# Two more theta tiles on split operands, under a new written-out order, in an attention and mixing kernel

## The chip, the cores and the metric

The kernel runs on one core of a Trainium2 chip. The metric is the device time of one execution in microseconds. Five engines work side by side, each through its own list of instructions in a fixed order: TensorE (PE, with its weight loads shown as PEld), VectorE (DVE), ScalarE (ACT), GpSimd (POOL), and SyncE (SP), which here only issues DMAs. An instruction starts when the one before it on its engine has left and the semaphores that it waits for have come.

## The reference

The first half is an attention over a sliding window and over block sums; the second half mixes its result along the sequence and along the channels. With 4 batches, 8 heads, 768 positions and 64 values per head, `x` is 768 x 512 per batch:

```python
    k_sum = k.reshape(B, H, nb, block, D).max(axis=3)      # block = 32
    v_sum = v.reshape(B, H, nb, block, D).mean(axis=3)
    scores_l = scale * np.matmul(q, k.transpose(0, 1, 3, 2))  # kept where |s - t| < 16
    scores_s = scale * np.einsum('bhsd,bhnd->bhsn', q, k_sum) + np.log(block)
    ...                                       # softmax over both, times v and v_sum
    theta = x @ w_theta
    zr, zi = x * np.cos(theta), x * np.sin(theta)
    y = np.einsum('ts,bsd->btd', w_tok_r, zr) + np.einsum('ts,bsd->btd', w_tok_i, zi)
    u = x + y
    return u + np.maximum(u @ w_ch, 0.0)
```

Everything is float32 in the result. The weights arrive as float64 and are made into float32 on the chip.

## The kernel before, in words

**Tiles.** Each batch has six tiles of 128 positions, so there are 24 tiles, numbered 0 to 23; batch 0 has tiles 0 to 5. For each tile the kernel does in turn: scores on PE (L538), mask, scale and row minimum on DVE (L574, eight pairs of instructions), exponentials on ACT (L578, eight), transposes of the result on PE (L587), their copies to SBUF on ACT or DVE (L593), the product with the values on PE (L561), and its normalisation (L602 to L611), which gives `xn`, the tile of `x`. Then `x` is turned: for the first six tiles by PE transposes (L638), later through DRAM. Then comes theta (L672 or L677), its reduction to one turn and cosine and sine (L688 to L701), and the product with `x` (L707), called `zu`.

**Two ways to multiply.** A float32 product of full precision is done raw (L672), with float32 operands, in which each matmul shows as two records in the trace; or on split operands (L677): each operand is cast to a rounded part (the high part, L311 or L313) and the rest is kept as a second part (the low part, a subtraction, L320), and three matmuls high x high, high x low, low x high take the place of the raw one. In the table `TUNE`, `RT` is the number of the first tile whose theta is done on split operands: 6 before. From that tile on, `x` of the tile is split into `xh` and `xl`. The split weights of theta, tiles `wth`, are made from the float32 weights, which lie until then in the same four buffers of the tags `xh` and `xl`.

**Mixing.** Each batch is mixed over the sequence in six steps for each half of the channels: raw for the first four steps of batch 0 (L735 with the operand `zu`), on split operands (L735 with `hl`) until batch 1 is done, and for batches 2 and 3 by a scheme with seven products in the place of eight (L851). The channel product of all batches ends the program (L956), with its sums on DVE (L963) and the final relu and sum (L975), each of which is stored.

**Order.** Nothing is scheduled on the chip or by the compiler. The kernel records some 2330 operations, and `ORDER`, a written-out list of their numbers, gives the one order in which all of them are issued; the letter behind a number (p, a, d, g) chooses PE, ACT, DVE or POOL where an operation can run on more than one, and without a letter the cheapest by the kernel's own costs is taken. Each engine runs its instructions in that order. All DMAs go through the one queue of SP, also in that order, and one that waits for a buffer holds up all behind it. An instruction of POOL that the kernel marks with `port` also waits for the last marked instruction of DVE, if that was issued just before it among the marked ones.

Of the kernel before, what the change touches and what calls it, by code (L numbers as in the profile page):

```python
# [54 lines left out]
27 23 25 15 31 39 17 24 29 99 44 28 33 0g 1g 2 35 78 3 45 4 186 40 85 26 193 43 8g 5 6g 9 30 10 11g 18 19 7g 194 20 21 22 32  # L55
12 48g 47 14 46 49 50 13 190g 237g 100 101g 34 239 59 63 235 51 60 52 64 61 65 238g 192 36 92 54 58 56 53 79 55 102 62 187 57
103 37 38g 104 105d 66 691d 67 80 81 82 42g 188g 83 191 68 195 41 291g 69d 70 196 189g 240g 84 71 86 87g 293 199 106 107 198
197 204 206 294g 207 200 203 205 685g 241 72 75d 289 73 210 76 208 74d 202 77d 88 93 223 236 201 211 209 347g 242 245 249 94
224 243 244 345g 247 89 212 213 215 214 246 225 248 216 117 95 220 90 96 91d 97 346g 250 397 348g 98 226 217d 251 252 108 253
218 221 254 227 256 219d 118g 292g 222d 122 119 228 123 255 258 257 124 229 230 689g 120 259 260 295 261 296 269 121 262 419g  # L60
125 231 109 298 270 263d 232 302 126 233 398 266 343 264 271 304 405 272 687g 273 274 290 399 128 692g 307 267 281 265d 311
268d 275 297 306 110 282 305 299 421g 301 309 276 349 285g 300 303 310 406 308 129g 350 352 234g 353 312 130 277 354 131 313
283 323 315 400 111 416 314 133 316 351 358 409 324 325 420 418 284 360 287g 278 317 362 134g 355 135 356 364 132 326 136 327
357 359 363 137 328 279g 344 401 288g 280 361 365 329 320d 403 422 318 321 319d 322d 410 431 366 367 138 686g 434 438 330 433
335 368d 337 331 417 377 688g 402 432 601g 369 332 404 378d 370 116 139g 338 476 690g 423 426 430 477 371d 374d 424 372 437
375 379 425 429 373d 376d 380 140 411 381 334 407 141 428 142 286g 113 16 427 439 436 435 527 440 441 442 478 602 382 172
333g 412 443 383 479 482 408 528 447d 444d 487 445 489 336 143 491 389 144g 448 112 384 173g 446 449d 488 524 486 490 153 413
494 493 145 414 174 146 492 114 391 450 473 483 480 484 481 485 415g 529 147 495 525 115 148 390 175 385 526 392 149g 386 154
475 127 451d 530 474 150 496 155 497 151 498 452 176 453 454 455 152 156 158 387 157 456 499 177 727 533 457 500 532 388g
503d 572 501 504 159g 178 538 458 459 502d 464 460g 506 466 540 505d 165 467 507 539 508 693 509 537 531 535 510 536 543 534  # L70
160 541 542 545 694 544 697 511 695 728 166g 167 179 462 512 161 546 547 168 573 162 169 696 463g 465 163 180 698 549 513 170
548d 164 514 515 699 181 171 550 182 516 518 608 522 554 183 523 700g 393 519 520 184 729 521 574 551 517g 575 561 341g 607
582 584 394g 576 461g 559 731 588 701 555 702 185 585 730 637 571 580 560 733 562 557 719 552 553 577 558g 732 579 581 703
1238 563 583 556 768 578 713g 734 569 565 771 589 586 342 609 339g 340g 769 590 587 720 567 591 592 704 564 638g 735 593 603
468g 736 1239 770 594 595 618 705 706 621 610 611 615 470 620 772 598 1240 613 617 612 1241 625 599 721 722 469g 773 723 395g
396 774 596 622 597d 600 604 800 624 605 639 606 641 642 619 647 640 645 775g 776 616 614 626 623 627 643 714 650 724 725
471g 679g 629d 568 644g 824g 628 651 630 566 802 803 707 472 631 632 825 708 634d 801 660 826 661 827 828g 829g 739 652 655
804 805 726 662 777 649 635 737g 710 666 709 646 656 653 681 654 680 682 658 778 779 780 830d 633 648 683 684 832 636d 781
715 947 716 711g 659 570 664 831 657 668 665 977 806 663 834g 667 807 669 835 833 670 836g 740 981 671d 672 673d 738 980 717
837g 838 712 808 839 978 741 979 782 783 844 749 809 948 718 750 982 676 840 842 745 944 945d 785 752 784 674 677 756 753  # L80
841g 743 1028g 742 675d 678 810 811 812 744 748 746 983g 984g 788 751 843 790 813 755 791 1242 845 747 1001 814 754 757 758
760 815 1002 796 759d 786d 949 846 761 765 789 787 1003 958 959 963 854g 961 965 950 855g 762d 962 763 792 985 1005 816 951
856g 1004 794 798 766 1029 986 987 988 952 820 954 953 1243 989 990 797 817g 847g 848 818d 849g 1006 819 764d 955 960 991 767
992 946 850d 793 1007d 957 821 822 1087 823 997 1058 964 998 999 1008 1009 1000 956 966 967 969 852 1023 1030 1061 1059 968
1060 970 994 851 864g 865g 853 857 858 1062 1021 1025 993 995 859 860g 866 867 1010 1039 1022 1031 861g 799 795 1034 1011 971
1063 862 1042 1024 1038 1032 1036 1033 1137 974 1043 972 1035 1041 973d 868 869g 975 976d 1214 870g 1045 1040 1012 1037 1026
1046 1047 1064g 1065g 863 1044 1048 1050d 1027 1013 1049 1014 1088 1051 1215 871 1015 1089 1218 1091 1216 996g 874g 875 1066
1016 1052d 1086 1217 1017g 1093 873 1097 1099 1055d 1053 1056 1019g 1020g 1100 872 876g 1103 1067 1068 1069 1095 1219 1070
1092 1220g 1018 1101 1090 1094 1080 1081 1098 1054d 1136 1096 1078 1079 1102 877g 1246 1057d 1287 1104 1105 1106 1107 1250
1138 1082 1083 1290 1288 1071 1072d 1108 878 1109 1247 1289 1221g 1166g 1222 1073 1074 1110d 1113 1114 1076d 1223 1147 1224  # L90
1225 1291 1292 1151 1075g 1226 1251 1111 879g 1252 1139 1084 1142 1141 1112 1085 1077 1148 1248 1293d 1294g 1227 1140 1115
1317 1253 1120 1143 1118 1116 1179 1130 1144 1119 1249 880 1150 1146 1258 1149 1121 1128 1167g 1145 1154 1295 1296 1254 1255
# [83 lines left out]
class Program:  # L176
# [5 lines left out]
    WINDOW, WARM, COOL = 3.41, 0.88, 0.45  # L182
# [971 lines left out]
```

## Time and profile before

| what | value |
|---|---|
| median of 3 runs | 426.37 us |
| the 3 runs | 426.08, 426.37, 429.6 us |
| the profiled execution | 425.32 us |
| its span, first to last instruction | 423.6 us |
| PE busy | 413.3 us, 98% of the span |
| PE weight loads busy | 343.9 us, 81% |
| DVE busy | 356.3 us, 84% |
| ACT busy | 298.1 us, 70% |
| POOL busy | 207.4 us, 49% |
| DMA moved | 100.07 MB |
| granted TensorE clock | 1.000 |

A busy share is a mean over the whole span, and stages differ: a matmul's end is modelled and lies after the start of the next, so that PE reads as busy wherever matmuls follow each other without a pause.

### The profile page before, as it was taken

To read this page: it belongs to the slowest core of one execution; us is meant where nothing else is said; L and a number is where in the kernel's file an instruction comes from. 1 tells how busy PE (TensorE), PEld (TensorE's weight loads), DVE (VectorE), ACT (ScalarE), POOL (GpSimd) and SP (SyncE) were. 2 spreads that over 40 slices of the span, in tenths; PEclk is the share of its full clock that TensorE was granted. 3 is DMA by queue.
4 is the path that set the end of the run, shared out by engine and by line. 5 is a ranking of instruction groups with operands and counts; after the bars stand their busy time and mean duration, and the time that the engine had idled before them with its cause. 6 is when DMAs were issued, how large, how long until landed. Compare 5 with 4: busy or idle time off the path is not lost.

```text
span 423.6 us, 10058 instructions
## 1 busy us (share of the span) xinstructions
PE 413.3 (98%) x3626; PEld 343.9 (81%) x3626; DVE 356.3 (84%) x963; ACT 298.1 (70%) x609; POOL 207.4 (49%) x211
## 2 busy tenths in 40 slices
PE   8789999999999999999999999999999999999996
PEld 3356666578888888888888899898889999999996
DVE  3799999998797896787778787776887899999996
ACT  2899999997588886878779976685564547465230
POOL 3435562329833545875755876835515411133241
PEclk9999999999999999999999999999999999999999
DMA  8999799567869799777896998998788599111355
GB/s 294 351 351 319 256 384 285 157 212 193 273 181 245 177 261 277 223 241 230 227 271 166 310 248 244 303 267 249 182 242 336 192 349 305 50 39 45 124 209 183
DMA packets 95234, 100.07 MB, mean 236 GB/s; under 512 B 41936, under 2 KB 80848, under 8 KB 95184
## 3 DMA queue, kind: packets, MB, share of 16 engines
q1 hardware_dynamic: 95184, 99.43, 76.0%
q8 instruction: 28, 0.46, 0.4%
q14 instruction: 22, 0.18, 0.1%
HBM read 75.82 MB, written 23.59 MB: 235 GB/s over the span
## 4 chain that ended last, share of the span: by engine, by line
PE 88%; DVE 7%; ACT 2%; issue 1%; DMA 1%; DVEq 0%; SPq 0%; ACTq 0%
PE m L735 23%; PE m L851 20%; PE t L677 11%; PE c L956 6%; PE pa L561 6%; PE m L956 5%; PE s L538 5%; PE t L672 4%; PE pa L587 3%; PE t L381 2%; PE t L956 1%; DMA v<-vg 1%; DVE e L574 1%; DVE x L975 1%; DVE f L763 1%
## 5 line engine op out<-in xcount | busy, mean ns | idle before, releaser
L851 PE MATMUL m<-wt,hl 128*128 128x384 f32 x504 | 93.0, 339 | 0.3
L851 PEld LDWEIGHTS m<-wt,hl 128*128 128x128 f32 x504 | 87.2, 188 | 3.5 <-issue 0.5
L735 PE MATMUL m<-wt,hl 128*128 128x512 f32 x480 | 89.4, 340 | 0.0
L735 PEld LDWEIGHTS m<-wt,hl 128*128 128x128 f32 x480 | 74.2, 188 | 11.6 <-issue 0.3
L578 ACT ACTIVATE e<-e,st 128x118 f32<-128x118 f32 x192 | 64.4, 389 | 10.6 <-DVE st L574 7.3
L574 DVE CUSTOM_DVE_ANT_0 e<-s,cs 128x118 f32<-128x118 f32 x192 | 45.6, 271 | 7.1 <-PE pa L561 4.5
L320 POOL TENSOR_TENSOR hl<-zu,hl 128x512 fp32r<-128x512 f32 x24 | 33.1, 1386 | 27.8 <-ACT hl L311 8.5
L677 PE MATMUL t<-wth,xh 128*128 128x512 f32 x144 | 45.8, 399 | 0.0
L707 POOL TENSOR_TENSOR zu<-xn,zu 128x512 f32<-128x512 f32 x24 | 32.9, 1381 | 21.2 <-DVE wt L414 10.0
L311 ACT CAST hl<-zu 128x512 fp32r<-128x512 f32 x43 | 26.1, 619 | 16.4 <-PE m L851 9.9
L561 PEld LDWEIGHTS pa<-v,e 118*64 118x64 f32 x768 | 24.6, 137 | 9.7 <-issue 3.4
L320 DVE TENSOR_TENSOR hl<-zu,hl 128x512 fp32r<-128x512 f32 x38 | 28.3, 751 | 3.0 <-ACT hl L311 2.9
L561 PE MATMUL pa<-v,e 118*64 118x65 f32 x768 | 28.0, 224 | 2.7 <-ACT xh L1031 1.0
L677 PEld LDWEIGHTS t<-wth,xh 128*128 128x128 f32 x144 | 25.2, 188 | 4.5
L677 PE MATMUL t<-wth,xl 128*128 128x512 f32 x72 | 28.4, 394 | 0.0
L763 POOL TENSOR_TENSOR zu<-zu 128x512 f32<-128x512 f32 x14 | 18.8, 1357 | 16.2 <-DVE hl L320 10.9
L763 POOL TENSOR_TENSOR f<-f 128x192 f32<-128x192 f32 x26 | 17.4, 670 | 18.2 <-DVE f L763 11.2
L538 PE MATMUL s<-k 64*64 64x118 f32 x768 | 25.7, 266 | 0.6 <-PE pa L561 0.6
L593 ACT COPY e<-pa 118x512 f32<-118x512 f32 x30 | 16.7, 584 | 13.4 <-PE pa L587 13.4
L578 ACT ACT_TABLE_LOAD x18 | 23.1, 1283 | 2.7 <-DVE st L574 2.5
L700 ACT ACT_TABLE_LOAD x19 | 24.4, 1283 | 0.3
L593 DVE COPY e<-pa 118x512 f32<-118x512 f32 x18 | 12.2, 688 | 14.5 <-PE pa L587 8.4
(181 smaller groups left out, 891.0 us busy)
## 6 DMA issues: line engine op xcount, KB each, us to landing
wt<-s_scratch SPq DMA_DIRECT2D x48, 384.0 KB, 5.1
k<-qg SPq DMA_DIRECT2D x18, 632.0 KB, 5.7
v<-vg SPq DMA_DIRECT2D x24, 390.0 KB, 5.5
s_scratch<-f SPq DMA_DIRECT2D x24, 384.0 KB, 3.5
wt<-wtr SPq DMA_DIRECT2D x6, 768.0 KB, 10.5
wt<-wti SPq DMA_DIRECT2D x6, 768.0 KB, 11.7
f<-kT SPq DMA_DIRECT2D x12, 384.0 KB, 3.6
f<-vT SPq DMA_DIRECT2D x12, 384.0 KB, 4.8
```

Of the source, the lines that this page charges most:

```text
L320: lambda e: V[e].tensor_tensor(dst(), src(), hi().bitcast(F32), op=ALU.subtract), reads, writes, due, port=BOTH)
L538: mm(0.79 * len(pairs) / NP, [lambda p=p, g=g, h=h: nc.tensor.matmul(sc[h].get()[ROW[g], p], q()[ROW[h], p, ROW[g]], keys_of()[ROW[h], :, ...
L561: mm(2 * 0.433 + scores[0] + (0.2 if scores[0] else 0.0), [lambda n=n, g=g, a=a: nc.tensor.matmul(xa[a].get()[ROW[g], n], turned[g].get()[ ...
L574: op({"DVE": 0.205}, lambda eng, n=n: nc.vector.tensor_tensor_reduce(e()[:, n], sc[n % 2].get()[:, 2 * a + n // 2], mask(m), -SCALE, 3.0e3 ...
L578: op({"ACT": 0.288}, lambda eng, n=n: nc.scalar.activation(e()[:, n], e()[:, n], AF.Exp, bias=st.get()[:, n:n + 1], scale=-1.0), [(st, n)] ...
L593: lambda e, t=t, g=g: (nc.scalar.copy if e == "ACT" else nc.vector.tensor_copy)(t.get()[:NK], tp[g].get()[:NK].rearrange("k n q -> k (n q) ...
L677: calls = [lambda t=t, xx=xx, k=k, c=c: nc.tensor.matmul(th.get(), xx.get()[:, c], w_th[c].get()[:, k], start=(c == 0 and t == 0), stop=(c ...
L707: op({"DVE": c_dve(DM, "two"), "POOL": c_pool(DM)}, lambda e, z=z, hc=hc: V[e].tensor_tensor(z(), xn[b, i].get().rearrange("p h d -> p (h ...
L735: nc.tensor.matmul(acc[th](), zz, w[:, TT[th]], start=(s == 0 and r == 0 and t == 0 and (th == 0 or c == 0)), stop=(s == NT - 1 and r == 1 ...
L763: lambda e: V[e].tensor_tensor(dst(), x(), y(), op=ALU.add if sign > 0 else ALU.subtract), reads, writes, due, port=BOTH)
L851: calls = [lambda ref=ref, tt=tt, z=z, s=s, j=j, t=t, x=x, k=k, bank=bank, first=first: nc.tensor.matmul(bank[j].get()[:, :HT], z.get()[:, ...
L956: calls = [lambda k=k, t=t, x=x, y=y: nc.tensor.matmul(to.get(), weights[n][x][0]()[:, k, j * P:(j + 1) * P], operands[n].get()[:, y, k], ...
```

## The change

`RT` goes from 6 to 4: theta of tiles 4 and 5 (the fifth and sixth of batch 0) is done on split operands, as that of all later tiles already was. Each of the two loses four raw matmuls (eight records) and gets twelve on split operands, one cast and one subtraction. All of `ORDER` is written anew (two of its lines are shown), with four more numbers, 2336 in place of 2332; nothing else in the file differs. A few operations change their engine with it: of the 48 multiplications of L707, 24 stood on DVE and 24 on POOL, and 30 and 18 stand there now; ACT gets 36 table loads in place of 38. The number of DMAs, 317, is the same.

```diff
 ORDER = """
-27 23 25 15 31 39 17 24 29 99 44 28 33 0g 1g 2 35 78 3 45 4 186 40 85 26 193 43 8g 5 6g 9 30 10 11g 18 19 7g 194 20 21 22 32
...
+27 17 31 23 25 14 0 29 1g 8 9 10 2 3 15 16 4 5 13 39 44 33 18 19 20 21 48 35 78 186 45g 40 85 99 24 26 43 28 11g 30 46g 194g
...
 TUNE = dict(R_W2=0.0, PS_T=1, XHB=2, FB=3, FC=2, R_M=49.3, R_C=20049.4,
             R_W=72.0, R_PRE=-11.25, R_KV=14.48, R_SM=-38.05, R_AV=27.7, R_TH=-7.23, R_Z=16.22, R_Z2=-31.01, R_X=0.0, XT=1, XNB=3, A0=3,
-            A1=13, T1=10, PREP=5, VSPE=1, VB=2, KB=2, STR=2, WARM=5, SP0=1, FUSE=99, RELOAD=2, RT=6, RM=4, XA=6, XB=2, ZU=5, HL=4, EB=3, TAU_A=8.2, TAU_M=4,
+            A1=13, T1=10, PREP=5, VSPE=1, VB=2, KB=2, STR=2, WARM=5, SP0=1, FUSE=99, RELOAD=2, RT=4, RM=4, XA=6, XB=2, ZU=5, HL=4, EB=3, TAU_A=8.2, TAU_M=4,
```

The first place is the head of SP's queue, the loads with which the program begins (`kT` and `qg` hold keys and queries, `vn` the values for the block sums, `wth` the raw weights of theta, `vg` the values). Before:

```order
L305 DMA zu<-kT 128x798 x3
L305 DMA x<-vn 128x2x512
L305 DMA k<-qg 128x512
L305 DMA zu<-kT 128x798
L305 DMA wth_91<-wth 128x1024
L305 DMA x<-vn 128x2x512 x2
L305 DMA wth_103<-wth 128x1024
```

Now:

```order
L305 DMA zu<-kT 128x798
L305 DMA x<-vn 128x2x512
L305 DMA zu<-kT 128x798 x3
L305 DMA k<-qg 128x512
L305 DMA x<-vn 128x2x512 x2
L305 DMA wth_123<-wth 128x1024
```

The last of the four key loads moved up from sixth to fifth place, and the second and third load of `vn` stand ahead of the first weights.

The second place is the head of ACT's list. Before:

```order
L506 ACT_TABLE_LOAD
L506 COPY k<-zu 128x47x2x2 x3
L519 COPY k<-ks 128x12x2x2 x2
L506 COPY k<-zu 128x47x2x2 x2
L519 COPY k<-ks 128x12x2x2 x2
L403 ACTIVATE xl<-wth_91 128x512
L506 COPY k<-zu 128x47x2x2
L578 ACTIVATE e<-e,st 128x118 x3
```

Now:

```order
L374 ACT_TABLE_LOAD
L374 ACTIVATE loaded<-beps 128x1
L506 COPY k<-zu 128x47x2x2 x2
L519 COPY k<-ks 128x12x2x2 x2
L506 COPY k<-zu 128x47x2x2 x3
L578 ACTIVATE e<-e,st 128x118 x6
```

The first table load now belongs to an operation that needs no DMA, and the first conversion of weights (L403) moved behind the first exponentials. On PE, which has no rows here, the scores of tile 1 moved ahead of the transposes of tile 0 (they stood behind them), and the product with the values of tile 0, the turning of its `x` and the transposes of tile 1 now follow each other, with the scores of tile 2 behind them (these stood ahead of the turning).

The third place is PE at theta of tile 4. Before, behind the transposes of tile 6 (the last row of which stands first):

```order
L587 MATMUL pa_1025<-cs,e 118x64
L672 MATMUL t<-xh,x 128x512
L672 MATMUL t<-xl,x 128x512
L672 MATMUL t<-xh,x 128x512
L672 MATMUL t<-xl,x 128x512
L561 MATMUL pa_1087<-v,e 64x65 x8
```

Now, behind the scores of tile 7:

```order
L538 MATMUL s_1059<-k 64x118
L677 MATMUL t<-wth_417,xh 128x512 x2
L677 MATMUL t<-wth_417,xl 128x512
L677 MATMUL t<-wth_465,xh 128x512 x2
L677 MATMUL t<-wth_465,xl 128x512
L677 MATMUL t<-wth_700,xh 128x512 x2
L677 MATMUL t<-wth_700,xl 128x512
L677 MATMUL t<-wth_498,xh 128x512 x2
L677 MATMUL t<-wth_498,xl 128x512
L735 MATMUL m_629<-wt,zu 128x512
```

Four raw matmuls became twelve on split operands; theta of tile 5 is changed in the same way.

## Rows read from the trace of the kernel before

**Rows 1.** Page, busy time of each engine, its share and its instructions.

```profile
PE 413.3 (98%) x3626; PEld 343.9 (81%) x3626; DVE 356.3 (84%) x963; ACT 298.1 (70%) x609; POOL 207.4 (49%) x211
```

**Rows 2.** Windows: length, then busy time of PE, PEld, DVE, ACT, POOL, clock, DMA.

```profile
0.00:30.00 30.00, 24.50 (x225) 11.78 (x226) 20.60 (x85) 19.74 (x53) 12.28 (x37) 1.00 0.96 328
30.00:90.00 60.00, 59.46 (x604) 35.72 (x604) 58.31 (x169) 58.73 (x117) 28.20 (x28) 1.00 0.82 275
90.00:120.00 30.00, 30.00 (x303) 25.08 (x300) 25.75 (x70) 21.25 (x53) 21.38 (x18) 1.00 0.84 238
120.00:355.00 235.00, 234.36 (x2131) 206.84 (x2130) 187.56 (x541) 170.11 (x343) 124.36 (x116) 1.00 0.84 248
355.00:424.00 69.00, 65.01 (x374) 64.53 (x373) 64.05 (x103) 28.26 (x48) 21.20 (x12) 1.00 0.35 122
```

**Rows 3.** Chain that ended last: start, length in us, what; theta tiles on PE.

```profile
72.93 3.65 PE t L672 x8
...
145.15 2.79 PE t L677 x12
...
168.97 3.00 PE t L677 x12
```

**Rows 4.** Waits of PE over the span: total us, times, longest.

```profile
PE t L381 <- DVE zu L379: 1.6, 1, 1.6
PE pa L561 <- ACT xh L1031: 1.0, 1, 1.0
PE pa L561 <- DVE e L593: 0.9, 2, 0.5
PE pa L587 <- ACT vs L475: 0.8, 1, 0.8
PE pa L561 <- issue: 0.6, 1, 0.6
PE s L538 <- PE pa L561: 0.6, 1, 0.6
PE pa L452 <- DMA x<-vn: 0.4, 1, 0.4
PE t L672 <- ACT x L311: 0.4, 1, 0.4
```

**Rows 5.** Timeline of PE in the head: start, length, instruction, [idle before].

```profile
12.41 3.61 PE L452 MATMUL pa<-x,vt 128*24 128x512 f32 x8 [0.44 <-DMA x<-vn]
16.80 0.68 PE L587 MATMUL pa<-cs,e 64*118 64x64 f32 x16 [0.77 <-ACT vs L475]
17.40 1.08 PE L538 MATMUL s<-k 64*64 64x118 f32 x32
19.45 1.24 PE L561 MATMUL pa<-v,e 118*64 118x65 f32 x32 [0.97 <-ACT xh L1031]
21.24 1.48 PE L538 MATMUL s<-k 64*64 64x118 f32 x32 [0.55 <-PE pa L561]
```

**Rows 6.** Timeline of ACT in the head.

```profile
6.18 1.28 ACT L506 ACT_TABLE_LOAD   x1 [6.18 <-DMA zu<-kT]
...
17.71 0.57 ACT L593 COPY e<-pa 118x512 f32<-118x512 f32 x1
```

**Rows 7.** Groups by line and shape: busy us, mean ns | idle before, releaser.

```profile
L707 DVE TENSOR_TENSOR zu<-xn,zu 128x512 f32<-128x512 f32 x24 | 19.4, 817 | 3.6 <-ACT zu L701 3.5
L611 DVE TENSOR_TENSOR xn<-pa,st 128x256 f32<-128x256 f32 x35 | 13.8, 415 | 1.9 <-POOL zu L707 1.6
L604 DVE RECIPROCAL st<-st 128x4 f32<-128x4 f32 x48 | 7.6, 170 | 0.4
L320 POOL TENSOR_TENSOR xl<-x,xh 128x512 fp32r<-128x512 f32 x8 | 10.6, 1321 | 11.4 <-DVE f L414 4.8 <-DVE st L574 2.1 <-DVE f L763 1.8
L707 POOL TENSOR_TENSOR zu<-xn,zu 128x512 f32<-128x512 f32 x24 | 32.9, 1381 | 21.2 <-DVE wt L414 10.0 <-ACT zu L701 4.9 <-DVE hl L320 4.7
L311 ACT CAST xh<-x 128x512 fp32r<-128x512 f32 x11 | 6.8, 615 | 2.0 <-DMA x<-t_scratch 2.0
```

More of the change, by code (lines that the diff above doesn't have):

```diff
@@ L59 @@
[L59 to L92, printed above, removed]
@@ new lines @@
+204 73 101g 208 76 74d 77d 205 209 198 202 207 206 210 88 102 236 211 93 94g 293 89 223 212 213 224 241 103 214d 215 397 216
+225 292 90 91 104 226 105 95 128 250 254 129g 220 96 217d 450g 97 98 227 252 242 246 245 243 244 249 218 251 247 130 253 248
+255 221 219d 222d 256 228 257 258 348 346g 259 452g 347g 229 345g 131 295 418g 230 117 261 132 456g 304 260 231 306 310 269
+262 270d 398 266d 343 271 272 305 232 421g 118g 307 296 300 298 299 297 457g 273 119 233g 303 349 274 107 290 301 263d 120
@@ new lines @@
+393 1242 734 570g 573 571 591 572 598 339 723 575 776 774 574 581 773 577 602 341g 775 603 604 579 1243 614g 342g 340 621 630
+739 605 1246 631 740 615 606 529g 622 623 710 625 711d 627 724 616 617 633 777 651 741g 395 396 619 618 634 626 576 652 629
+635 778 610 725 653 712 779g 394 632 636 729 1247 611 662 655 714g 607d 608 609 612d 624 478g 727 726 828g 713 804 743 730
+829g 628 806 479 480d 657 691d 692 780 781 830 782 728 637 783 784 808 658 638 807 639 654 641 656g 785 663 640 642 661 646
@@ new lines @@
+1261 1411g 1267 1207 904 905g 1272 1209 1210 1271 1180 1133 1181 912g 1213g 1276 1208d 1268 1216 1217 1408 1211d 1215 1238
+1333 1390 1409g 1274 1265 1269 1239 1275 1279 1270 1334 1273 1335 906 1277 1344 1394 1336 1391 1278 1280 1281 1283 1393 1615g
+1392 913 1378d 1379 1380 1381 1382 918g 919 907 1412 1395 1627 920g 1282 1345 1284 1383 1309 921 1310 914 1337g 1410 1240
+1241 1621 1348 1352 1346 1349 1347 1351 1396 922g 1285d 915g 1397g 1286 1338 1709 1287d 1384 1385 1350 1288 1289 1628 1290d
+1441 923g 1622 1386 1387 916 1706 928g 929 930g 917 1398 1339 1341 1311 1312 1313 1444 1353 1356 924d 1357 1355 1354 1358
@@ new lines @@
+1485d 1496 1488 1601 1493 1495 1636g 1707 1710 937 946 1501 947 1637 1794 1494 1723 1711 1503 1507 1505 1497 1498 1559 1638
+1602 1603g 1643 1499 1604g 1560 1714 1642 1713 1715 1720 1508 1509 1511 1521 1726 1561 1510d 1645d 1562 1729 1512 1797 1648g
+1522 1524 1716 1717 1732 1563 1564 1516d 1735 1719 1517 1796 1530 1526 1534 1605 1606 1718 1519 1722 1525 1646g 1725 1795
+1653g 1654g 1529 1523 1527 1647 1649d 1528 1568 1721 1724 1727 1607 1651g 1608 1609 1565 1650g 1798 1533 1513d 1537 1754
+1657g 1728 1760 1730 1531 1535 1514 1731 1734 1610 1566g 1666g 1737 1652 1733 1763 1739 1799 1736 1611 1532 1741 1743 1766
@@ L143 @@
+2274 2287 2275 2301 2270 2284 2302 2316 2296 2297 2288g 2322 2323 2268 2299 2320 2250 2317 2191 2290 2292 2298 2300 2291 2271
+2304 2308 2303 2318 2324 2305 2293g 2251 2319 2325 2306 2309 2310 2321 2326 2327 2208 2272 2307 2329 2330 2311 2328 2331 2332
+2333 2334 2335 2312 2313 2314
 """
```

116 lines of the change are left out of this document (66 added, 50 removed), and 3 rows, old and new, of the table ORDER.

## The prediction, made before the changed kernel had run

> **What bounds the kernel now.** I read the page's engine line first [rows 1]: PE is busy for 413.3 of 423.6 us, DVE for 84%, ACT for 70%. A share over the whole span hides stages, so next came the busy time by window [rows 2], and there the reader is to see three things. In the first 30 us PE works 24.50 us, so 5.5 us are idle. From 30 to 90 us PE has 59.46 of 60 us, but DVE (58.31) and ACT (58.73) are as full: three engines are at their limit together, while POOL has 28.20. From 90 us on PE stays full (30.00 of 30, 234.36 of 235) and DVE and ACT have room (DVE 25.75 of 30, 187.56 of 235). In the last window the idle 4 us are the end, with the last sum and its store; the last product is the same in the new order, so I leave the end as it is.
>
> The waits of PE [rows 4] sum to 6.3 us. 1.6 us is the start, 3.8 us lies in the head, and only the two waits on the copy L593 (0.9 us) lie later. So after 30 us a time is gained almost only by giving PE less to do, and lost by any wait that the new order brings. The granted clock is 1.00 in every window, that is 2.4 GHz.
>
> **The change, part by part.**
>
> *Theta of two tiles, on PE.* The chain shows what one tile costs either way [rows 3]: raw theta of tile 4 took 3.65 us in 8 records, a tile on split operands 2.79 us in 12 where it follows mixing, and 3.00 us where it follows a product with the values. The saving is 0.65 to 0.86 us for a tile, 1.3 to 1.7 for both. Tile 4 now follows scores and tile 5 mixing, so I take 0.7 and 0.85: **-1.6 us** (a sum of 1.55, rounded). PE's own queue gains this only if nothing else ends last there, which is the first rival's question.
>
> *What pays for it elsewhere.* Each of the two tiles adds a cast of `xh` on ACT (615 ns) and a subtraction for `xl` on POOL (1321 ns) [rows 7]: 1.2 us on ACT and 2.6 us on POOL. POOL is at 28.20 of 60 us, so its part is hidden as long as it comes in time. In the new order `xl` of tile 4 stands some 13 us of PE work ahead of its theta (the transposes of tile 5, mixing, theta of tile 3, a product, four more pieces of mixing and scores), that of tile 5 some 10 us, against a chain of turning, copy, cast and subtraction that I put at about 4 us with its hand-overs (an estimate: 615 + 1321 ns of these rows, twice for the copy and what waits ahead). ACT has no such room from 30 to 90 us. But the new order has two table loads fewer by then, each 1.28 us [rows 6], so ACT's sum falls by 1.3 us there. I put both at 0; if the cover failed, each tile would hold PE for at most its 2 us. The four split weights must also be ready earlier, by theta of tile 4 in place of tile 6; they were all made before that point in the old order too, so 0.
>
> *The head.* Term by term from the timeline [rows 5]. The 0.44 us for `vn` should go, since its loads stand ahead of the first weights now. The 0.77 us for the copy of the block sums (L475) is covered by the scores of tile 1, 1.08 us, which moved ahead of the transposes. The 0.97 us ahead of the first product with the values stays nearly whole: its copies (0.57 us on ACT [rows 6]) now follow the transposes with nothing between, though no longer behind weight conversions; -0.1. The 0.55 us ahead of the scores of tile 2 and the 0.4 us for `x` ahead of theta [rows 4] lose their cause, because that work is now further from what it needs. Against this stands a new wait: the turning of tile 0 follows the product directly and needs the normalisation, about a reciprocal and two multiplications on DVE, 170 + 2 x 415 ns [rows 7], with hand-overs about 1.2 us. Sum -0.44 - 0.77 - 0.1 - 0.55 - 0.4 + 1.2 = **-1.0 us**, with ends at -2.3 (no new wait) and +1.2 (all old waits stay). The table load, 1.28 us, no longer begins after the first keys have landed [rows 6]; it lets ACT start earlier, and I count it as what makes these numbers possible, not a second time.
>
> *Changes of kind on PE.* The small matmuls (scores, transposes, products) cost something where PE enters or leaves them: 3.00 against 2.79 us [rows 3], 0.21 us. Counted over the whole order, PE's list has 182 runs of one kind in place of 191. At 0.21 us that would be 1.9 us, but part of the nine is the theta above and part is a cheaper change in place of a dear one: **-0.4 us**, between -1.9 and 0.
>
> *DVE from 90 to 120 us.* Up to the scores of the eleventh tile (tile 10, at 117 us before) the new order has eleven more DVE instructions and four fewer, beside small fills: subtractions for split operands, a reduction, a multiplication, two normalisations. At 817 ns for an added and 415 ns for a dropped one [rows 7] that is 7.3 us; at 415 ns for all, 2.9 us. I take 6, because most of the added ones are full tiles. DVE was idle there for 30 - 25.75 = 4.25 us [rows 2], so 1.75 us do not fit. Not all of that is needed by PE at once: **+0.6 us**, between 0 and 3.0 (7.3 - 4.25). Six multiplications that moved from POOL (1381 ns) to DVE (817 ns) [rows 7] add 4.9 us to DVE, nearly all after 120 us, where it has 47 us of room: 0.
>
> Later waits of PE, 0.54 + 0.64 us [rows 2], may go or others come: 0, within 1.2 us either way. DMAs are the same in number; that those of the later stages were moved I price at 0, since PE never waited for a transfer after the head [rows 4].
>
> **Sum:** -1.6 - 1.0 - 0.4 + 0.6 = -2.4 us on the profiled execution's 425.32, so 422.9. That execution lies 1.05 us below the median of the runs, 426.37; on the median it is **424.0 us**.
>
> **The rivals.**
>
> *The saving is not on the path: 426 us.* From 30 to 90 us DVE and ACT are as full as PE; if what they hold ends last, PE merely waits for the 1.6 us saved and only the head is left, part of it lost again in the same stage. For it: 58.31 and 58.73 of 60. Against it: theta's saving comes with two table loads fewer, so ACT falls as well, and PE's idle time there is 0.54 us. The Trainium skill speaks for this rival: Perfetto Trace Analysis, Identifying the Most-Contended Engine, says that matmul busy time is no measure of PE's headroom, and to go by the weight loads' share. By that rule PE would be only 60% used there (35.72 of 60 [rows 2]), PE would have 24 us to spare, and theta's term would be 0. The trace does not bear it out for this stage: the raw matmuls, two long records for a load, give few loads while they follow each other without a gap. Chance 0.20.
>
> *DVE becomes the bound from 85 to 120 us: 428.3 us.* This is the case on the other side. If DVE's idle time there is made of waits for PE's and ACT's results, it cannot take the added work; with a quarter of it usable, 6.0 - 1.1 = 4.9 us late, less the 3.0 us gained, +1.9. It decides from the point where DVE's list is more than 3.0 us behind PE's: the summing of the accumulators (L754) and the subtractions ahead of mixing then hold PE. For it: 58.31 of 60 just before, so DVE enters the stretch without a reserve. Against it: POOL has room, and in the first 90 us DVE's list is some 2 us shorter. Chance 0.15.
>
> *The order is as good as PE alone allows: 420.5 us.* All waits of PE after the start go (6.3 - 1.6 = 4.7 us), with theta 1.6: -6.3, less some 0.4 that any hand-over leaves. For it: PE is the only full engine for 330 us. Against it: the new wait in the head. Chance 0.13.
>
> The forecast itself, 422.6 to 425.4 us, has 0.52. That the change is not what it says is excluded by the order's rows: the twelve matmuls stand there for both tiles.
>
> **Range and chances.** 421.0 to 428.3 us holds the forecast, the first rival, half of the second and a third of the third. 1% is 4.3 us, about what a measurement of this kernel tells from no change. Faster by over 1% (below 422.1) takes the third rival and nothing else: 0.12. Slower by over 1% (above 430.6) takes the far end of the second: 0.04. Within 1%: 0.84.
>
> **What the new profile would show.** Theta of tiles 4 and 5 in 12 records of about 2.8 us each, and PE's windows after 30 us still full. In the head: no wait on `vn` or on L475, and a wait of about 1 us ahead of the first turning (L638). DVE fuller than 25.75 us from 90 to 120. PE waiting for L320 or L754 between 85 and 120 us would show the second rival; a PE idle time from 30 to 90 us that grew by 1 to 2 us, the first. I am wrong about the mechanism if PE is full, theta is shorter and the span is still not shorter by about 2 us, which would mean that mixing's matmuls or their changes cost more than counted.

## The result, and the profile after

The change made the kernel slower: 430.0 us, the median of 20 runs, against 426.57 us of 20 runs of before beside them, a ratio of 1.0067 (95% interval 1.0049 to 1.0085; the ratios here are estimated from the single runs and differ a little from the quotient of the medians). In a second comparison, with 12 runs, it was 1.0052 (1.0028 to 1.0076). I had forecast 424.0 us with a range up to 428.3; within 1% held, the sign did not. The profiled execution took 429.39 us, 4.07 more than the 425.32 of before.

The page's engine line, to be read against [rows 1]:

```profile
PE 415.4 (97%) x3634; PEld 347.6 (81%) x3634; DVE 357.9 (84%) x963; ACT 298.6 (70%) x604; POOL 207.1 (48%) x209
```

The busy time by window, columns as in [rows 2]:

```profile
0.00:30.00 30.00, 25.88 (x226) 13.69 (x226) 20.73 (x88) 19.42 (x53) 12.29 (x35) 0.89 0.97 321
30.00:90.00 60.00, 58.60 (x615) 37.04 (x615) 57.37 (x168) 58.11 (x119) 30.76 (x32) 1.00 0.89 278
90.00:120.00 30.00, 28.91 (x233) 24.33 (x232) 27.84 (x70) 23.55 (x48) 17.79 (x15) 1.00 0.74 222
120.00:355.00 235.00, 232.87 (x2167) 203.75 (x2166) 185.60 (x535) 164.46 (x334) 123.85 (x118) 1.00 0.83 245
```

PE is no longer full after 30 us. In the three windows behind the head it was idle for 0.54, 0.00 and 0.64 us; now it is for 1.40, 1.09 and 2.13. The mean clock of the first window is 0.89 where it was 1.00. The waits of PE, against [rows 4]:

```profile
PE pa L561 <- ACT e L593: 1.5, 4, 0.6
PE t L381 <- DVE zu L379: 1.5, 1, 1.5
PE pa L561 <- ACT vs L475: 1.1, 1, 1.1
PE t L638 <- DVE xn L611: 0.9, 1, 0.9
PE s L538 <- DVE xl L411: 0.8, 1, 0.8
PE pa L561 <- POOL v L501: 0.8, 1, 0.8
PE m L851 <- DMA wt<-s_scratch: 0.6, 1, 0.6
PE pa L561 <- DVE e L593: 0.5, 1, 0.5
```

The waits on `vn` and on L475 ahead of the transposes are gone, as forecast; others stand in their place, 3.1 us of them ahead of products with the values (L561) from tile 2 on. One is a wait for a transfer (`wt<-s_scratch`, at 345 us; 1.2 us in the second trace of the change), of which the first trace of before has none and the second 0.3 us.

**Where the time went.** There are points at which both orders have given PE the same work, but for theta's own saving. The starts in PE's timelines give the delay there, against the trace of before, in us (33: product of tile 2; 105: product of tile 8; 269: scores of tile 22; 369: the second block of the last product, L956):

| kernel | 33 us | 105 us | 269 us | 369 us |
|---|---|---|---|---|
| before, a second trace | -0.1 | -0.1 | -0.1 | 0.2 |
| the change | 0.2 | 1.2 | 3.8 | 4.3 |
| the change, a second trace | -0.2 | 0.2 | 2.7 | 3.6 |

My sum asked for -1.0 at 33 us, some -2.2 to -2.4 at 105 us, and no more after that. Against that sum the two traces of the change lost 1.2 and 0.8 us in the head, 1.6 to 2.4 from 33 to 105 us, and 2.6 and 2.5 from 105 to 269 us, where I had booked nothing; another 0.5 and 0.9 came from 269 to 369 us.

### The profile page after: what moved, and what is told of

The parts are those of the page before. It is cut to its first block, busy times and chain, and to the rows that moved or that the text cites. A ratio compares the mean times of both kernels' runs of the same rounds, so it can differ in the third digit from the quotient of the medians.

```text
span 427.7 us, 10049 instructions
## 1 busy us (share of the span) xinstructions
PE 415.4 (97%) x3634; PEld 347.6 (81%) x3634; DVE 357.9 (84%) x963; ACT 298.6 (70%) x604; POOL 207.1 (48%) x209
## 4 chain that ended last, share of the span: by engine, by line
PE 76%; ACT 11%; DMA 6%; DVE 3%; issue 2%; SPq 1%; POOL 0%; ACTq 0%; POOLq 0%; DVEq 0%
PE m L851 20%; PE m L735 17%; PE t L677 11%; PE c L956 7%; PE m L956 6%; PE pa L561 5%; PE s L538 4%; PE pa L587 2%; ACT e L578 2%; DMA wt<-wti 2%; PE t L672 2%; DMA wt<-s_scratch 1%; ACT L700 1%; DMA zu<-kT 1%; ACT e L593 1%
## 5 line engine op out<-in xcount | busy, mean ns | idle before, releaser
L677 PE MATMUL t<-wth,xh 128*128 128x512 f32 x160 | 50.9, 399 | 0.0
L320 POOL TENSOR_TENSOR hl<-zu,hl 128x512 fp32r<-128x512 f32 x22 | 29.5, 1342 | 27.8 <-DVE f L414 8.9
L561 PEld LDWEIGHTS pa<-v,e 118*64 118x64 f32 x768 | 25.7, 141 | 10.8 <-issue 3.5
L707 POOL TENSOR_TENSOR zu<-xn,zu 128x512 f32<-128x512 f32 x18 | 24.9, 1387 | 17.3 <-ACT zu L701 6.4
L561 PE MATMUL pa<-v,e 118*64 118x65 f32 x768 | 29.4, 228 | 3.9 <-ACT e L593 1.5
L677 PEld LDWEIGHTS t<-wth,xh 128*128 128x128 f32 x160 | 28.6, 188 | 5.5 <-issue 0.2
L320 DVE TENSOR_TENSOR hl<-zu,hl 128x512 fp32r<-128x512 f32 x40 | 30.3, 759 | 3.2 <-POOL hl L313 2.8
L677 PE MATMUL t<-wth,xl 128*128 128x512 f32 x80 | 31.4, 393 | 0.0
L538 PEld LDWEIGHTS s<-k 64*64 64x64 f32 x768 | 20.7, 134 | 8.0 <-issue 3.7
L707 DVE TENSOR_TENSOR zu<-xn,zu 128x512 f32<-128x512 f32 x30 | 22.6, 768 | 5.0 <-ACT zu L701 5.0
L593 ACT COPY e<-pa 118x512 f32<-118x512 f32 x34 | 19.2, 582 | 10.7 <-PE pa L587 8.7
L320 POOL TENSOR_TENSOR xl<-x,xh 128x512 fp32r<-128x512 f32 x13 | 18.6, 1433 | 14.6 <-ACT xh L311 9.7
```

Source lines behind the costliest of these rows:

```text
L320: lambda e: V[e].tensor_tensor(dst(), src(), hi().bitcast(F32), op=ALU.subtract), reads, writes, due, port=BOTH)
L538: mm(0.79 * len(pairs) / NP, [lambda p=p, g=g, h=h: nc.tensor.matmul(sc[h].get()[ROW[g], p], q()[ROW[h], p, ROW[g]], keys_of()[ROW[h], :, ...
L561: mm(2 * 0.433 + scores[0] + (0.2 if scores[0] else 0.0), [lambda n=n, g=g, a=a: nc.tensor.matmul(xa[a].get()[ROW[g], n], turned[g].get()[ ...
L593: lambda e, t=t, g=g: (nc.scalar.copy if e == "ACT" else nc.vector.tensor_copy)(t.get()[:NK], tp[g].get()[:NK].rearrange("k n q -> k (n q) ...
L677: calls = [lambda t=t, xx=xx, k=k, c=c: nc.tensor.matmul(th.get(), xx.get()[:, c], w_th[c].get()[:, k], start=(c == 0 and t == 0), stop=(c ...
L707: op({"DVE": c_dve(DM, "two"), "POOL": c_pool(DM)}, lambda e, z=z, hc=hc: V[e].tensor_tensor(z(), xn[b, i].get().rearrange("p h d -> p (h ...
```

## The experiments

The tables give each kernel's ratio to before with its interval, and its trace's delay at the four points. Line numbers in the experiments' rows are 3 or 4 higher than in the change, because their order has fewer or more rows. A number in `ORDER` is one operation.

### The split operands or the order?

```diff
 # order_alone: the order of the change
-RT=4   ... 460 461g 518 519g ...
+RT=6   ...
 # theta_alone: the order of before
-RT=6
+RT=4   ... 459 460 461g ...   (copy of tile 4 moved from DVE to ACT, cast, low part)
+       ... 517 518 519d ...   (tile 5: cast on ACT, low part on DVE)
 # theta_later: theta_alone, and
-460 461g 490 ... 149g 386
+460 490 ... 149g 461g 386
```

> The order of the changed kernel without the split operands of tiles 4 and 5 (they stay on float32, the four added operations left out). First theory, the new order loses the time: the loss of 3.4 us plus the 1.6 us that the split operands no longer save, so about 431.6 us, ratio 1.012, and the granted clock falls to 0.5 near 20 us as in the changed kernel. Rival, the split operands lose it: about 426.6 us, ratio 1.000, and no fall of the clock.

> Tiles 4 and 5 of theta on split operands as in the change, in the order of before, with the four new operations put in (both casts on ScalarE, the low part of tile 4 on GpSimd, that of tile 5 on VectorE). First theory, the split operands save what the prediction gave them and the new order loses the time: 1.6 us below before, so about 425.0 us, ratio 0.996, granted clock 1.00 throughout. Rival, the casts and the subtraction cost more on full engines than TensorE saves: 428 to 430 us, ratio 1.003 to 1.008, with the waits of the head's products longer on ScalarE or VectorE.

> The split operands in the order of before, as in the first of these experiments, with one operation elsewhere: GpSimd's low part of tile 4 behind two short operations (a memset of 0.10 us and a weight step of 0.83 us) that in the first trace waited for it, with VectorE idle 3.4 us behind them. If the split operands gain what TensorE saves once that wait is gone: 1.0 to 1.6 us below before, ratio 0.996 to 0.998. If ScalarE and VectorE bound the stage, so that TensorE's saving is not on the path: ratio 0.999 to 1.002. If their added 1.2 and 0.7 us are paid in full: ratio 1.003 to 1.005.

| kernel | ratio | 33 us | 105 us | 269 us | 369 us |
|---|---|---|---|---|---|
| order_alone | 1.0107 (1.0069 to 1.0146) | -0.2 | 1.2 | 3.8 | 4.1 |
| theta_alone | 1.0109 (1.0069 to 1.0148) | 3.6 | 7.6 | 7.5 | 7.6 |
| theta_later | 1.0103 (1.0072 to 1.0133) | 0.7 | 6.2 | 6.3 | 6.5 |

Both theories were half right. The new order alone loses about 4.6 us by its ratio. The split operands in it seem to give some of that back (1.0107 to 1.0067 or 1.0052, 1.7 to 2.4 us), but the intervals overlap, and by the traces it is less: from 33 to 105 us order_alone loses 1.4 us, the change 1.0 and 0.4. In the order of before the same split operands lose as much as the new order does, and all of it between 33 and 105 us: 3.9 us in the first trace and 5.6 in the second, in which the clock fell at 95 us (last section); what theta_alone shows at 33 us is a late head and a fall of the clock from 20.9 to 27.7 us. Moving GpSimd's low part away, on which I had put the blame, did not help. PE's timeline of theta_later shows the wait, and DVE's what it waits for:

```profile
90.11 1.56 PE L739 MATMUL m<-wt,zu 128*128 128x512 f32 x4
93.94 1.15 PE L565 MATMUL pa<-v,e 118*64 118x65 f32 x32 [2.27 <-DVE e L597]
```

```profile
88.66 1.82 DVE L415 SCALAR_TENSOR_TENSOR f<-wt,f 128x768 int32<-128x768 int32 x2
90.40 1.82 DVE L418 SCALAR_TENSOR_TENSOR f<-wt,f 128x768 uint32<-128x768 uint32 x2
92.13 0.55 DVE L411 TENSOR_SCALAR f<-f 128x768 f32<-128x768 f32 x1
92.60 0.68 DVE L694 SCALAR_TENSOR_TENSOR zu<-zu,t 128x512 f32<-128x512 f32 x1
93.20 0.68 DVE L597 COPY e<-pa 118x512 f32<-118x512 f32 x1
```

DVE works through weight conversions without a gap and reaches the copy at 93.20, when PE has been ready for a while. In before, PE waited for this same copy for 0.54 us:

```profile
89.19 1.15 PE L561 MATMUL pa<-v,e 118*64 118x65 f32 x32 [0.54 <-DVE e L593]
```

DVE ended last there already, and 1.7 us of what ACT and DVE got more came out at this copy. Five shorter waits between 70 and 85 us, for ACT and DVE, made up another 1.7 us. In that order PE's saving did not reach the end.

### The clock

In the trace of the change the granted clock fell to 0.5 (1.2 GHz) from 19.9 to 26.8 us; in before's, and in the second trace of the change, it stayed at 1.00 there. The eleven small matmuls of the next kernel stand in PE's waits ahead of that:

```diff
+    blank = Ref(pm, [P, 512], tag="m2")
+    for n in range(11):
+        pr.key = ("FILL", n)
+        mm(0.22, [lambda: nc.tensor.matmul(blank.get()[:, :P], ident(), ident(), start=True, stop=True)], ...)
```

> The changed kernel with eleven small matmuls on constants (their products are never read, 0.22 us each) put into TensorE's waits of the head: three ahead of the product with the values of tile 0, four ahead of the turning of tile 0, four ahead of the scores of tile 2. If TensorE's idle time there is what lets the granted clock fall: clock 1.00 throughout, and about 1.8 us back less what the small matmuls take beyond the waits, 428.2 to 428.7 us, ratio 1.004 to 1.005. Rival, the clock falls for another reason: it still falls near 20 us, and the time is 430 us or more, ratio 1.008 and up.

The ratio is 1.0057 (1.0035 to 1.0079), with delays of 0.7, 0.2, 2.8 and 3.2 us. Stretches of 5 us, of the change and then of this kernel:

```profile
15.00:20.00 5.00, 3.28 (x83) 2.72 (x82) 4.70 (x19) 4.65 (x13) 2.91 (x5) 0.99 1.04 376
20.00:25.00 5.00, 4.20 (x58) 3.19 (x59) 4.98 (x18) 4.83 (x13) 1.56 (x3) 0.50 1.03 297
```

```profile
15.00:20.00 5.00, 5.00 (x93) 3.85 (x92) 4.36 (x18) 4.67 (x13) 2.37 (x4) 1.00 1.01 339
20.00:25.00 5.00, 4.37 (x65) 3.29 (x63) 5.00 (x17) 4.71 (x13) 2.23 (x4) 1.00 1.04 275
```

With PE busy, the clock stayed, in all twelve runs (0.998 to 1.000). The time was that of the change: 0.0005 above its second comparison, 0.0010 below the first. While the clock is at half, DVE (4.98 of 5) and ACT (4.83) are nearly full, so that one would expect a slower PE mostly to wait less.

But the equal time does not show that a fall is free, because the small matmuls have a price as well. Behind the last of them the scores of tile 2 start at 23.72 us; in the second trace of the change, without them and without a fall, at 22.80 us. The traces with this head bear that out. From the scores of tile 1 to the product of tile 2, the four without a fall there (after_again, order_alone, pe_mend, early_mend) lose 1.2 to 1.3 us against before; the four with a fall of 6.8 us (the change, mend_late, early_mend2, pe_mend_d) lose 2.4 to 3.5 us; three with one of 3.4 us (mend_all, early_new, till_s22) 1.4 to 2.5; this kernel, without a fall, loses 2.3. So a fall of 6.8 us goes with 1.1 to 2.2 us, and the small matmuls cost about 1 us (an estimate from these differences).

The runs agree. Those of the change with a mean clock of 1.000 were 2.0 us faster than the rest (four runs, 428.66, against sixteen, 430.66), and of 105 runs of before beside the experiments the 85 at 0.998 or above have a median of 426.95 us, the other 20 one of 428.45. Since 16 of the 20 runs of the change lie below 0.998, the clock seems to have a share in the loss, which no experiment separates. It is not the main part: early_new (next section) lies below 0.998 in ten of its twelve runs and comes out near before, late_new in two of six and comes out no better than the change.

### Which half of the order?

At the turning of tile 7's exponentials (86 us) the two orders have nearly the same work behind them, so they can be joined there.

```diff
 # early_new (RT=4): up to the turning of tile 7 the order of the change, behind it that of before
-... 558 559 | the rest of the change
+... 558 559 | 162 169 473g 475 163 180 702 561 525 170 560d ...
 # late_new (RT=6): the other way round
```

> The kernel before, unchanged, for a trace of it beside the experiments: in their traces the fourth to ninth transfer of SyncE's queue take 0.5 to 1.4 us each to issue where the first trace of before had 0.45 to 0.7, and the first scores come up to 0.8 us later. If that comes from the occasion and not from the experiments' code, this trace shows such slow issues too, with scores of tile 1 at 18 us or later (17.4 in the first trace). If it comes from the code, the issues take 0.45 to 0.7 us and the scores of tile 1 start at 17.4 us.

> The changed kernel, unchanged, beside the next three on the same chip, so that they are compared with it and with before at once. Its ratio to before was 1.0067 (1.0049 to 1.0085); the same here if the experiments' ratios of 1.010 and more were their own, 1.010 or more if it was the occasion's.

> Split operands; the order of the change up to the turning of tile 7's exponentials (86 us), the order of before from there on (the two orders have nearly the same work done there: six operations are ahead, four behind). If the loss lies behind 90 us, as TensorE's idle time in the traces has it (4.6 of 12.4 us in the changed kernel against 1.1 of 6.4 before): about 3 us below the changed kernel, ratio to before 0.999 to 1.002. If it lies ahead of 90 us: no different from the changed kernel.

> The other half: theta of tiles 4 and 5 on float32 and the order of before up to the turning of tile 7's exponentials, the order of the change from there on. If the loss lies behind 90 us: 3 to 3.5 us above before, ratio 1.007 to 1.008. If it lies ahead of 90 us: ratio 1.000.

| kernel | ratio | 33 us | 105 us | 269 us | 369 us |
|---|---|---|---|---|---|
| after_again | 1.0052 (1.0028 to 1.0076) | -0.2 | 0.2 | 2.7 | 3.6 |
| early_new | 1.0011 (0.9986 to 1.0035) | 0.7 | 1.2 | 1.6 | 1.6 |
| late_new | 1.0088 (1.0060 to 1.0116) | 0.7 | 2.4 | 4.6 | 5.7 |

This is the clearest result: the new order behind 86 us, on top of before's head and float32 theta, carries a loss as large as the change's, and the new head with the split operands costs next to nothing. At the join itself late_new has 0.4 us of idle PE (91 us). before_again ran once (425.59 us): its head was 0.8 us late at the scores of tile 1 and had caught up at 33 us.

An earlier join at the first mixing step (old_head: the order of before up to there, the new one behind) came out at 1.0247. Its trace has a wait of 4.9 us at the join, which is its own, so it tells nothing of the change.

> Split operands for tiles 4 and 5; the order of before up to the first mixing step, the order of the change from there on. First theory, the head of the new order loses about 1.8 us through the fall of the granted clock and the rest is lost later: clock 1.00, about 428.5 us, ratio 1.005. If all of the loss lay in the head: about 425.0 us, ratio 0.996. If the head loses nothing, the clock's fall included: 430 us, ratio 1.008.

### Are the waits the price?

Two places behind 86 us stand out, tiles 8 and 13. Read at points of equal work (times of before), the loss is not spread: from 90 to 105 us, ahead of the product of tile 8, the two traces of the change lose 1.2 and 0.8 us; from 149 to 175 us, where the product of tile 13 lies, 2.1 us each; in all the rest from 105 to 269 us, 0.5 and 0.4. late_new loses 1.6 and 2.1 us at these two places and order_alone 1.1 and 2.1, while early_new, with before's order there, loses nothing at either. The chain of waits of the change from 100 to 106 us, ahead of tile 8's product (start, length, what):

```profile
99.84 0.72 DVE e L621
...
102.12 2.82 DMA t_scratch<-e
...
105.08 0.58 ACT e L593
105.67 0.49 ACT vs L475
```

Tile 7's transposed result lies in the buffer that tile 8's second copy (L593) will overwrite; its transfer landed at 104.94, and the copy and then L475 follow one another on ACT. In before that transposition was no earlier (100.50 us), but both copies of tile 8 ran from 102.79 us and waited for no transfer. At tile 13, PE, ACT and DVE:

```profile
170.78 0.97 PE L587 MATMUL pa<-cs,e 64*118 64x64 f32 x16
171.68 1.32 PE L735 MATMUL m<-wt,hl 128*128 128x512 f32 x6
173.48 0.33 PE L561 MATMUL pa<-v,e 118*64 118x65 f32 x2 [0.48 <-DVE e L593]
174.38 1.15 PE L561 MATMUL pa<-v,e 118*64 118x65 f32 x30 [0.58 <-ACT e L593]
...
171.32 1.28 ACT L700 ACT_TABLE_LOAD   x1
172.62 0.72 ACT L700 ACTIVATE zu<-zu,bright 128x512 f32<-128x512 f32 x1
173.25 0.61 ACT L701 ACTIVATE zu<-zu 128x512 f32<-128x512 f32 x1
173.77 0.56 ACT L593 COPY e<-pa 118x512 f32<-118x512 f32 x1
...
171.21 0.95 DVE L320 TENSOR_TENSOR f<-f 128x768 fp32r<-128x768 f32 x1
172.74 0.68 DVE L593 COPY e<-pa 118x512 f32<-118x512 f32 x1
```

The turning (L587) is done at 171.7, but both copies queue, on ACT behind a table load and the sine, on DVE behind work on weights. Before, the copy followed the turning at once:

```profile
166.23 0.68 PE L587 MATMUL pa<-cs,e 64*118 64x64 f32 x16
166.84 1.04 PE L538 MATMUL s<-k 64*64 64x118 f32 x32
167.81 1.15 PE L561 MATMUL pa<-v,e 118*64 118x65 f32 x32
...
167.01 0.59 ACT L593 COPY e<-pa 118x512 f32<-118x512 f32 x1
```

Two ways to mend them (in the texts below, "the last" is the kernel before it in the diff):

```diff
 # mend_late: ACT's and DVE's lists
-738 588 ... 772 599 ... 739 605 1246 ... 740 615
+588 ... 772 738 599 ... 739 1246 ... 740 605 615
-869 865 1219 1019 870 871 872g 873g ... 1020 ... 1021g ... 1053d 1054 1055
+869 1219 1019 ... 1053d 1054 865 870 871 872g 873g 1020 1021g 1055
 # mend_all: mend_late, and
-117 261 ... 260 231 ... 287 497 ... 504 144 ... 441 145 146 442 288
+261 ... 260 117 231 ... 497 ... 144 ... 441 145 146 442 504 287 288
 # pe_mend: PE's list (pe_mend_d: also 504 and 287 as above)
-615 606 529g ... 616 617
+615 529g ... 616 606 617
-1054 1055 1059 1101 1070 1071 1072
+1054 1101 1070 1071 1055 1059 1072
```

> The changed kernel with two pieces of its order mended, each on ScalarE and VectorE, TensorE's order untouched: tile 7's transposition ahead of a reduction, and the copy of the means ahead of the second copy of tile 8's exponentials (TensorE waits 1.17 us there at 105 us); tile 13's two copies ahead of the sine step on ScalarE and of five operations on the weights on VectorE and GpSimd (TensorE waits 1.45 us there at 173 us). If the loss is the sum of such waits, each on the path: 2.3 to 2.6 us below the changed kernel, ratio to before about 1.001 (the changed kernel's is 1.007). Rival, the engines behind are full and the waits come back a little later: ratio 1.005 to 1.007, and other waits of the same sum in the trace.

> As the last, and two more pieces on ScalarE alone in the earlier stage: tile 2's copies ahead of one weight conversion, tile 5's copies ahead of one rounding and one exponential (TensorE waits 0.51 and 0.92 us there, at 33 and 63 us). If all of these waits lie on the path: 1.0 to 1.4 us below the last kernel, ratio to before 0.997 to 0.999. Rival, between 30 and 90 us ScalarE and VectorE are the bound (58.11 and 57.37 of 60 us busy), so what a copy gains another operation loses: no difference from the last kernel.

> The changed kernel with two moves on TensorE alone: the product of tile 8 with its values behind one more mixing step (1.3 us), that of tile 13 behind half of theta of tile 11 (1.8 us); what ScalarE, VectorE and GpSimd do keeps its order, but for the mean's scaling of tile 13 that follows its product. If TensorE's waits of 1.17 and 1.45 us there are on the path: about 2.5 us below the changed kernel, ratio to before 0.999 to 1.001 (the changed kernel's was 1.0052 and 1.0067). If the stage is bound by what feeds TensorE, the waits come back behind: ratio 1.005 to 1.007.

> The last with tile 5's copies on ScalarE ahead of one rounding and one exponential, which kept 0.4 us of a wait of 0.92 us at 63 us in two traces. If all three waits are on the path: 0.4 us below the last, ratio 0.998 to 1.000. Rival as for the last: 1.005 to 1.006.

| kernel | ratio | 33 us | 105 us | 269 us | 369 us |
|---|---|---|---|---|---|
| mend_late | 1.0103 (1.0077 to 1.0128) | 0.4 | 0.3 | 4.9 | 5.3 |
| mend_all | 1.0126 (1.0085 to 1.0166) | -0.5 | -0.1 | 4.5 | 5.4 |
| pe_mend | 1.0037 (1.0007 to 1.0066) | -0.7 | 0.5 | 1.6 | 2.2 |
| pe_mend_d | 1.0036 (1.0007 to 1.0065) | 2.6 | 3.0 | 4.2 | 6.4 |

The points of the table are the first matmul of a product. In pe_mend and pe_mend_d six matmuls of mixing, 1.3 us, were moved ahead of the product of tile 8, so 1.3 us of their delay at 105 us is work done earlier.

Moving copies ahead on ACT and DVE did not help. At tile 8 it did not even take the wait away: PE's waits of mend_late have

```profile
PE pa L564 <- ACT e L596: 2.8, 5, 1.4
```

and the longest, 1.43 us at 107 us, lies within the product of tile 8, behind its first two matmuls (the 0.3 us at 105 us of the table is read ahead of it). There the product waits for the second copy now, where it had waited 1.09 us for L475 behind that copy. At tile 13 PE's timeline has the product without a wait, and two other waits behind it:

```profile
173.82 1.15 PE L564 MATMUL pa<-v,e 118*64 118x65 f32 x32
...
184.63 0.50 PE L680 MATMUL t<-wth,xl 128*128 128x512 f32 x1 [0.50 <-POOL xl L323]
...
187.11 1.15 PE L564 MATMUL pa<-v,e 118*64 118x65 f32 x32 [0.37 <-ACT e L596]
```

From 149 to 186 us this trace loses 2.2 us, as much as the change. The sine was put off for the copies, and what hangs on it is late in its turn. Giving PE other work in the two waits did better, in pe_mend:

```profile
105.50 1.15 PE L564 MATMUL pa<-v,e 118*64 118x65 f32 x32
...
172.55 1.23 PE L564 MATMUL pa<-v,e 118*64 118x65 f32 x32
...
181.38 0.50 PE L680 MATMUL t<-wth,xl 128*128 128x512 f32 x1 [0.26 <-POOL xl L323]
```

Both products start without a wait. From 33 to 269 us, where all the moved work is done again, the trace loses 2.3 us; those of the change lose 3.6 and 2.9. By the ratios, too, pe_mend lies 0.6 to 1.3 us below the change, not the 2.5 expected, and the intervals overlap. So the waits seem to be in part on the path, and in part only to show that ACT, DVE and POOL deliver later there: behind tile 13 two waits of 0.26 and 0.39 us have come, and from 149 to 186 us pe_mend still loses 1.6 us. (pe_mend_d had a late head and a fall of the clock in the profiled run; its median is that of pe_mend.)

### Moving the join, and a better version

```diff
 # old_s16 (RT=6): joined at the scores of tile 16 (194 us), before's order ahead of it
 # till_s22 (RT=4): the order of the change up to the scores of tile 22 (270 us), before's behind it
 # early_mend: early_new with 504 and 287 behind 442;  early_mend2: early_mend, and
-162 169 473g 475 163 180 702 561 525 170 560d 164
+162 560d 169 473g 475 561 163 180 702 525 170 164
```

In the texts below, "the same" is late_new with a later join, and "the second" is early_new. An order joined at the product of tile 8 (105 us) has no time: its engines wait for each other in a ring. Its forecast, from late_new's ratio of 1.0088, was 1.005 if each place costs its wait, and 1.008 to 1.009 if the waits are one shortage.

> The same with the border at the scores of tile 16 (194 us). If each place costs its wait: only the 1.4 us behind 240 us is left, ratio 1.002 to 1.004. If it is one shortage: 1.007 or more. If the last place costs nothing: 1.000.

> The changed kernel up to the scores of tile 22 (270 us), the order of before from there on. If the stream of weights behind 240 us costs its 1.4 us: ratio 1.002 to 1.004, against 1.0052 and 1.0067 of the changed kernel. If not: 1.005 to 1.007.

> As the second, with tile 5's copies on ScalarE ahead of one rounding and one exponential (the mend that took TensorE's wait of 0.92 us at 63 us away in the trace of an earlier experiment, 0.4 us of which it kept until 90 us). If waits ahead of 90 us are on the path where they are not given back: 0.4 us below the second. If they are given back behind: no difference.

> The order of the change up to 86 us with tile 5's copies moved, that of before behind it, and tile 7's two copies ahead of one weight step on VectorE and one rounding on ScalarE (TensorE waits 0.93 us for VectorE's copy there, behind a chain of weight steps with no gap from 80 us on). If that wait is on the path and VectorE has room behind it: 0.9 us below the kernel without this mend, ratio 0.998. If VectorE is the bound from 80 to 95 us: the wait comes back at the next product that needs a converted weight, ratio 1.000.

| kernel | ratio | 33 us | 105 us | 269 us | 369 us |
|---|---|---|---|---|---|
| old_s16 | 1.0066 (1.0039 to 1.0093) | 0.7 | 0.6 | 2.7 | 3.5 |
| till_s22 | 1.0078 (1.0045 to 1.0110) | -0.3 | 0.5 | 3.1 | 4.0 |
| early_mend | 0.9998 (0.9973 to 1.0023) | -0.4 | 0.3 | 0.5 | 0.5 |
| early_mend2 | 1.0003 (0.9977 to 1.0028) | 0.7 | 1.1 | 1.4 | 1.9 |

The first two are inconclusive: old_s16 has 1.5 us of idle PE right at its join, till_s22 loses 1.0 us in the 16 us behind its own, as much as the step that each was to show. Which of the places behind 86 us costs how much therefore rests on the delays and idle times in the traces. The last two show that the good half of the change, with before's order behind it, comes back to the time of before; none of the kernels beats it. Neither of the two mends there shows a gain of its own: the intervals overlap with early_new's.

## Why the prediction was wrong, step by step

**Theta on PE: right.** The two tiles took 2.86 and 3.04 us in the change (73.95 to 76.81 and 81.77 to 84.81 us), 1.3 us less than the 3.65 and 3.53 before, against my 1.6.

**What pays for it elsewhere, booked at 0: wrong for the order of before, and not borne out in full for the new one.** In the order of before the cast, the copy and the subtraction cost 4 us or more, because work of DVE and ACT ended last, one copy on DVE above all. In the new order PE's idle time from 30 to 90 us grew by 0.9 us, and the traces show 0.4 to 1.0 us of theta's 1.3 at 105 us. This is the first rival's mechanism. By the rule I quoted for it (the Trainium skill, Perfetto Trace Analysis, Identifying the Most-Contended Engine) PE has headroom there; I set that against PE's idle time of 0.54 us and trusted the idle time. The rule was nearer: a PE that is busy for 59.46 of 60 us was not what ended last at that copy. The reason that I gave against the rule is wrong, too: the raw matmuls have a weight load for each record (48 and 48 of L672), and the load share is low because a load takes 0.19 us and a record 0.60.

**The head, -1.0 us: wrong, about 0** (0.2 and -0.2 at 33 us). PE's timeline there, against [rows 5]:

```profile
16.16 0.68 PE L587 MATMUL pa<-cs,e 64*118 64x64 f32 x16
17.62 1.26 PE L561 MATMUL pa<-v,e 118*64 118x65 f32 x32 [0.78 <-POOL v L501]
19.81 1.03 PE L638 MATMUL t<-cs,xn 128*128 128x128 f32 x4 [0.94 <-DVE xn L611]
20.78 1.32 PE L587 MATMUL pa<-cs,e 64*118 64x64 f32 x16
22.90 1.85 PE L538 MATMUL s<-k 64*64 64x118 f32 x32 [0.80 <-DVE xl L411]
```

The waits on `vn` and L475 went, the first product waits nearly as before, and the turning of tile 0 waits about as priced. What I had said would lose its cause, the wait ahead of the scores of tile 2, grew from 0.55 to 0.80 us under another name: a weight conversion on DVE stands ahead of what the scores need. And at half the clock the same sixteen matmuls take 1.32 us in place of 0.68, so that the product of tile 1 starts only 1.0 us earlier (24.7 for 25.7 us) where that of tile 0 was 1.8 earlier. The sum had no term for a fall of the clock. In the second trace, where it did not fall, the head still gained only 0.2 us.

**Changes of kind -0.4, DVE from 90 to 120 us +0.6: not measured apart.** DVE rose from 25.75 to 27.84 us there. The second rival's 428.3 us was nearest to the result, but its picture, PE waiting for L320 or L754, did not come: PE waited for ACT's L475 behind a copy, which stood behind the transfer of tile 7's transposed result.

**Later waits, "0, within 1.2 us either way": this is the step that failed.** The wait at tile 8 cost 0.8 to 1.2 us ahead of the point at 105 us, from 105 to 269 us the change lost 2.5 us, 2.1 of them around tile 13, and the join at 86 us showed that the loss is there: 1.0088 against 1.0011. I had read from the trace of before that PE hardly waits behind the head, and carried that over to an order in which every later place of every engine is another. The absence of waits was the property of that order, not of the stage: ACT was busy for 164 of 235 us and still could not turn a copy round in time when a sine stood ahead of it. The room that I saw in the windows says how much work fits, not when a given operation comes. The transfers, too, were priced at 0 because PE had never waited for one; in the new order it waits 0.6 and 1.2 us for `wt<-s_scratch` at 345 us.

What stays open is why the mended waits gave back so little, how much of the 2.1 us around tile 13 is the wait itself, and the clock's share in the loss.

## What to carry to other kernels

An order written out for the whole program is one object: a change that is local in what it computes moves every later hand-over, so where a bound engine owes its full list to the old order, price the new order's waits by the hand-overs themselves (what stands between a producer's input and the producer on its engine), not by the share of idle time. A saving on the fullest engine can be worth nothing where another engine's operation ends last, even with both at 97%, and then the extra work that pays for it shows in the time. When a wait has been found, try to give the waiting engine other work before reordering the engines that feed it (here that gave 0.6 to 1.3 us, not clear of the noise, and the other way nothing), and look whether the wait is really gone in the new trace; and join the old and the new order at a point where both have done the same work, to find the half that loses before explaining any wait.

## What was not expected of the hardware

The first transfers take unequal times to issue on SyncE's queue, with the same list. In before, and in theta_alone, which issues the same:

```profile
3.74 0.45 SPq L305 DMA_DIRECT2D wth<-wth  x1
4.23 0.97 SPq L305 DMA_DIRECT2D x<-vn  x2
```

```profile
3.94 1.38 SPq L309 DMA_DIRECT2D wth<-wth  x1
5.37 1.57 SPq L309 DMA_DIRECT2D x<-vn  x2
```

The scores of tile 1 came at 17.4 and 19.5 us, 18.2 in the second trace of before. So the head moved by up to 2 us between executions of the same list. The order of before took 0.8 us of it up in before_again (-0.1 at 33 us), and 0.6 of 1.4 us in late_new.

A fall of the granted clock to 0.5 for 6.8 us in the head went with 1.1 to 2.2 us there, although DVE and ACT were full for most of it. In theta_later the clock fell elsewhere, from 95.0 to 98.4 us, right behind PE's wait of 2.27 us, where mixing keeps PE busy: the first 25 matmuls of mixing took 6.23 us, while 36 of the same took 6.62 us in before, and that trace lost 1.7 us more from 33 to 105 us than theta_alone's, in which the clock stayed there.
